# Decode attention over a 65,536-row cache: V's loads issued from ACT's queue, K's from SP's

## The chip, the cores and the metric

The kernel runs on one core of one Trainium2 chip. The metric is the device time of one execution in microseconds (us); lower is better. Engines are named as in the profile: PE (matmul; PEld is its weight load), DVE (vector), ACT (scalar), POOL (GpSimd) and SP (sync). A "q" behind an engine's name is its sequencer, which issues instructions and transfers.

## The reference

One token is decoded by attention over a cache and by a gated feed-forward block; a gate mixes the two. All arrays are bfloat16.

```
x        (1, 1, 512)                 wq (512, 32*128)     wo (32*128, 512)
k_cache, v_cache  (1, 32, 65536, 128)                     gate_w (512)
w_gate, w_up (512, 1792)             w_down (1792, 512)

q = x @ wq, split into 32 heads of 128
for each head: p = softmax(q . K^T / sqrt(128)) over 65536 rows;  o = p @ V
a = concat(o) @ wo
b = (silu(x @ w_gate) * (x @ w_up)) @ w_down
g = sigmoid(sum(x * gate_w))
out = g * a + (1 - g) * b
```

K and V of one head are 16 MB each, and each byte is used once: 32 heads are 1074 MB.

## The kernel before, in words

**Tiles.** Each head's K and V are cut into two parts, u = 0 and u = 1. A part is 256 rows of the cache on each of 128 partitions, 64 KB a partition, 8 MB in all, and is one load (`place`). The text calls the parts of head h K_A(h), K_B(h), V_A(h) and V_B(h).

**Space.** All four lie in one buffer in SBUF, `ring`. K_A takes the bytes 0 to 64 KB of each partition and K_B 32 to 96 KB; V_A takes 96 to 160 KB and V_B 112 to 176 KB. The two parts of K share 32 KB, and those of V share 48 KB, so each load must wait until the part before it has been consumed far enough.

**One head.** DVE transposes a K part in 16 chunks (`turn`, L317) into one of four buffers `kt`, and counts them in the semaphore `ktd`. PE multiplies each chunk with q into `psS` (`scores`, L404) and counts in `qkd`. After both K parts DVE takes the maximum (L341), POOL spreads it over the partitions (L217), ACT forms the exponentials (`softmax`, L252 and L254) and copies the next head's q into `zq` (L259), and DVE transposes the result into `pb` (L343). Then PE multiplies V_A (`flow`, L420), rows 64 to 255 first, after which it raises `va1`. V_B's turn comes in the next head, behind the scores of K_A: PE's block `pe_vb` uses it (L420, then L455 and L411) and raises `vbd`; DVE helps in between (L330, L333) before it turns to K_B. In PE's program the order is thus K_A scores, V_B of the head before, K_B scores, V_A.

**Who issues the loads.** SP issues all of them, on its own queue: wq (L136), then three halves of head 0's K parts at once, then the last half after eight transposes (it carries `s_kb`; the text calls it kb) and V_A(0) (L165), all through the helper at L145. Then `head(r)` runs 31 times, the last time written out. Its waits are these:

- K_A(r+1) after eight transposes of K_B(r)
- V_B(r) after `va1`, which is raised in V_A(r)
- K_B(r+1) after eight transposes of K_A(r+1)
- V_A(r+1) after `vbd`, which is raised in V_B(r)

In the last of them wo is loaded ahead of K_B(31), in two halves, as K_A(31)'s space comes free. After it SP loads w_gate and w_up (once PE is through with wo, `s_wod`), w_down after the last transpose, and V_B(31) in six parts, the last five of them behind `va1`. PE's block `pe_wo`, between V_B(30) and the scores of K_B(31), works on wo; for it ACT copies `om` (L262).

ACT issues three transfers of 1 KB: x, gate_w and the result. `take_q(0)` is its copy of head 0's q (L233), as soon as the projections are through.

Of the kernel before, what the change touches and what calls it, by code (L numbers as in the profile page):

```python
# [9 lines left out]
K_A, K_B = 0, 32 * KB  # L10
V_A, V_B = 96 * KB, 112 * KB
# [15 lines left out]
def bass_gated_mix__mha_block_cached__swiglu_ffn__decode_kernel(  # L27
# [11 lines left out]
    out: bass.AP,  # L39
):  # L40
    _, H, S, Dh = A_k_cache.shape
    D = A_wq.shape[0]
    F = B_w_gate.shape[1]
    Dc = D // P
    FC = F // P
    ROWS = S // (2 * P)
# [8 lines left out]
    with ExitStack() as ctx:  # L55
# [6 lines left out]
        def sem(name):  # L62
            return ctx.enter_context(nc.semaphore(name))
# [47 lines left out]
        sm = {n: sem(n) for n in names.split()}  # L111
# [4 lines left out]
        kv_dram = {"k": A_k_cache[0].rearrange("h (u p r) d -> h u p (r d)", u=2, p=P),  # L116
                   "v": A_v_cache[0].rearrange("h (u p r) d -> h u p (r d)", u=2, p=P)}

        def at(byte, n):
            return ring[:, byte // 2:byte // 2 + n]  # L120
# [15 lines left out]
        nc.sync.dma_start(at(WQ, Dc * H * Dh), A_wq.rearrange("(p c) n -> p (c n)", c=Dc)).then_inc(sm["s_wq"], 16)  # L136
        nc.scalar.dma_start(xrow[0:1, :], xr_dram).then_inc(sm["s_x"], 16)

        body = ExitStack()
        block = body.enter_context(nc.Block())  # L140

        @block.sync
        def _(sp):
            def load(dst, src, s):
                sp.dma_start(dst, src).then_inc(sm[s], 16)  # L145

            def place(kind, h, u, s):
                byte = {"k": (K_A, K_B), "v": (V_A, V_B)}[kind][u]
                src = kv_dram[kind][:, u]
                if isinstance(h, int):  # L150
                    src = src[h]
                else:
                    src = src[bass.ds(h, 1)].rearrange("h p n -> (h p) n")
                load(at(byte, ROWS * Dh), src, s)

            k0 = kv_dram["k"][0, 0]
            k1 = kv_dram["k"][0, 1]
            half = ROWS * Dh // 2
            load(at(K_A + 2 * half, half), k0[:, half:2 * half], "s_ka")
            load(at(K_A, half), k0[:, 0:half], "s_k0a")  # L160
            load(at(K_B + 2 * half, half), k1[:, half:2 * half], "s_k0b")
            sp.wait_ge(sm["ktd"], NCH // 2)
            load(at(K_B, half), k1[:, 0:half], "s_kb")
            sp.wait_ge(sm["s_q"], 1)
            place("v", 0, 0, "s_va")  # L165

            def head(r, late):
                sp.wait_ge(sm["ktd"], r * PER + (PER - NCH // 2))
                place("k", r + 1, 0, "s_ka")
                sp.wait_ge(sm["va1"], r + 1)  # L170
                place("v", r, 1, "s_vb")
                if late:
                    wo_dram = A_wo.rearrange("(p j) n -> p (j n)", j=32)
                    for q in range(2):
                        sp.wait_ge(sm["ktd"], r * PER + (PER + 3 * NCH // 4 + q * NCH // 4))
                        load(at(WO + q * 16 * KB, 16 * D), wo_dram[:, q * 16 * D:(q + 1) * 16 * D], "s_wo")
                sp.wait_ge(sm["ktd"], r * PER + (PER + NCH // 2))
                place("k", r + 1, 1, "s_kb")
                sp.wait_ge(sm["vbd"], r + 2)
                place("v", r + 1, 0, "s_va")  # L180

            with nc.Fori(0, L - 1, engines=[ET.SP]) as i:
                head(i, False)
            head(L - 1, True)
            sp.wait_ge(sm["s_wod"], 1)
            load(at(WG, Dc * F), B_w_gate.rearrange("(p c) f -> p (c f)", c=Dc), "s_wg")
            load(at(WU, Dc * F), B_w_up.rearrange("(p c) f -> p (c f)", c=Dc), "s_wu")
            sp.wait_ge(sm["ktd"], PER * H)
            wd_dram = B_w_down.rearrange("(p c) n -> p (c n)", c=FC)
            load(at(WD, WD_CUT * D), wd_dram[:, 0:WD_CUT * D], "s_wd")  # L190
            last = kv_dram["v"][L, 1]
            for n, ((r0, r1), s) in enumerate(zip(PARTS, MARKS)):
                if n == 1:
                    sp.wait_ge(sm["va1"], H)
                load(at(V_B + r0 * 256, (r1 - r0) * Dh), last[:, r0 * Dh:r1 * Dh], s)
            for j, s in ((FC - 3, "s_wd1"), (FC - 2, "s_wd2"), (FC - 1, "s_wd3")):
                load(at(WD + 2 * j * D, D), wd_dram[:, j * D:(j + 1) * D], s)
# [25 lines left out]
        @block.scalar  # L223
        def _(act):
            chain = [0]

            def link(ins):
                chain[0] += 1
                ins.then_inc(sm["s_ach"], 1)
                act.wait_ge(sm["s_ach"], chain[0])  # L230

            def take_q(h):
                nc.scalar.copy(zq[:, :, 31:128:32], qd[:, h]).then_inc(sm["s_zq"], 1)  # L233

            act.dma_start(gwrow[0:1, :], gw_dram).then_inc(sm["s_x"], 16)
            act.wait_ge(sm["s_zb"], 1)
            nc.scalar.activation(sc[:, 1:2], psQ[:, 1, 0:1], ACT.Exp, scale=-1.0).then_inc(sm["s_e1"], 1)
            for b, bank in enumerate((psY, psZ)):
                act.wait_ge(sm["s_qr"], b + 1)
                nc.scalar.copy(qrow[:, b * D:(b + 1) * D], bank[:]).then_inc(sm["s_qc"], 1)  # L240
            act.wait_ge(sm["s_q"], 1)
            nc.scalar.copy(qTb[:], psM[:, 128:128 + H]).then_inc(sm["s_qTb"], 1)
            act.wait_ge(sm["s_qs"], 1)
            act.wait_ge(sm["s_qd"], 2)
            for g in range(4):
                link(nc.scalar.copy(qd[32 * g:32 * g + 32, :, :, g],
                                    psQ[32 * g:32 * g + 32, :, 0:H].rearrange("p e h -> p h e")))
            take_q(0)

            def softmax(h):  # L250
                act.wait_ge(sm["s_ar"], h + 1)
                nc.scalar.mul(nbias, amx, -SCALE).then_inc(sm["s_nb"], 1)  # L252
                act.wait_ge(sm["s_nb"], h + 1)
                nc.scalar.activation(pa[:], psS[:], ACT.Exp, bias=nbias, scale=SCALE,  # L254
                                     accum_out=rsum).then_inc(sm["s_exp"], 1)

            with nc.Fori(0, L, engines=[ET.Activation]) as i:
                softmax(i)
                nc.scalar.copy(zq[:, :, 31:128:32],  # L259
                               qd[:, bass.ds(i + 1, 1)].rearrange("p a e g -> p (a e) g")).then_inc(sm["s_zq"], 1)  # L260
            act.wait_ge(sm["s_o"], 1)
            nc.scalar.copy(om[:], psQ[:, 0, 0:32]).then_inc(sm["s_om"], 1)  # L262
            act.wait_ge(sm["s_wod"], 1)
            nc.scalar.copy(wo1_ap, psY[:]).then_inc(sm["s_woc"], 1)
            softmax(L)
            act.wait_ge(sm["s_h"], 1)
            nc.scalar.activation(hx[0], psY[:, 0:FW], ACT.Exp, scale=-1.0).then_inc(sm["s_sig"], 1)
            act.wait_ge(sm["s_y"], 1)
            nc.scalar.copy(brow[0:1, :], psF[0:1, :]).then_inc(sm["s_br"], 1)
            act.wait_ge(sm["s_y1"], 1)  # L270
            nc.scalar.copy(fin[0:1, D // 2:D], psZ[64:65, 0:D // 2]).then_inc(sm["s_fin"], 1)
            act.wait_ge(sm["s_fin"], 2)
            act.dma_start(out_dram, fin[0:1, :]).then_inc(sm["s_out"], 16)
# [294 lines left out]
```

## Time and profile before

| | us |
|---|---|
| median of 3 runs | 2513.6 |
| lowest and highest run | 2513.45, 2513.98 |
| the profiled execution's own time | 2514.02 |
| its span, first to last instruction | 2512.5 |
| PE busy | 1481.1 (59%) |
| DVE busy | 1249.7 (50%) |
| ACT busy | 43.0 (2%) |

In rows of the page's groups and of the timeline, L145 is the line of the kernel; `kt<-ring` says which tile is written from which; `x16` is a count. A row of the timeline begins with the start and the duration in us and ends, in brackets, with the idle time of the engine before it and what ended that. A row of the waits gives who waited for whom: the total in us, how often, the longest. A row of the queues gives packets, MB and the share of the 16 engines' time. A row of the DMA issues gives the count, at times the size, and the median time from issue to landing. The granted TensorE clock was 0.781 on the mean.

### The profile page before, as it was taken

What the parts mean: (1) busy time and instruction counts of PE and PEld (TensorE: products, weight loads), DVE (VectorE), ACT (ScalarE), POOL (GpSimd) and SP (SyncE); (2) the same over time, 40 slices, a digit from 0 to 9 for tenths busy, and PEclk for the clock granted to TensorE, in tenths of its full rate; (3) what the DMA queues carried; (4) which work ended last, traced back from release to release, by engine and by line L of the source; (5) the groups of instructions that cost most, each with busy time, mean ns of one, the idle gap of its engine ahead of it and who ended that gap; (6) DMA issues with size and microseconds to landing.
All of it is one profiled execution on the core that took longest, in us unless ns stands there. A gap on an engine that the chain in (4) does not pass through costs nothing.

```text
span 2512.5 us, 25156 instructions
## 1 busy us (share of the span) xinstructions
PE 1481.1 (59%) x10029; PEld 575.0 (23%) x10158; DVE 1249.7 (50%) x1213; ACT 43.0 (2%) x142; POOL 25.8 (1%) x81
## 2 busy tenths in 40 slices
PE   4664655645646546556465574564655655656568
PEld 1222222212212222222222221222222222222222
DVE  5463553644545536446455364464553644645534
ACT  0000000000000000000000000000000000000000
POOL 0000000000000000000000000000000000000000
PEclk8787877878778777777787787877877778778788
DMA  9999999999999999999999999999999999999999
GB/s 418 434 434 434 434 434 434 434 434 434 434 434 434 434 434 434 434 434 434 434 434 434 434 434 435 436 435 434 435 437 435 435 435 434 434 436 434 434 434 392
DMA packets 20746, 1087.71 MB, mean 433 GB/s; under 512 B 2307, under 2 KB 2694, under 8 KB 2950
## 3 DMA queue, kind: packets, MB, share of 16 engines
q1 hardware_dynamic: 20736, 1087.64, 100.0%
q8 instruction: 4, 0.07, 0.0%
q10 hardware_dynamic: 6, 0.00, 0.0%
HBM read 1087.64 MB, written 0.00 MB: 433 GB/s over the span
## 4 chain that ended last, share of the span: by engine, by line
DMA 75%; DVE 16%; issue 7%; PE 1%; DVEq 1%; SPq 0%; ACT 0%; POOL 0%
DMA ring<-in_A_k_cache_dram 74%; DVE kt L317 15%; PE psS L404 1%; DMA ring<-in_A_v_cache_dram 1%; DVEq L314 0%; SPq L145 0%; PE psW L420 0%; DVE st L328 0%; PE psY L426 0%; PE psO L411 0%; ACT pa L254 0%; DVE pb L343 0%; DVE st L341 0%; DVEq L327 0%; DVE fin L362 0%
## 5 line engine op out<-in xcount | busy, mean ns | idle before, releaser
L317 DVE STREAM_TRANSPOSE kt<-ring 128x1024 uint32<-128x1024 uint32 x1024 | 1163.2, 1206 | 932.4 <-DMA ring<-in_A_k_cache_dram 932.4
L404 PE MATMUL psS<-kt,zq 128*128 128x512 bf16 x3968 | 1103.3, 423 | 881.1 <-DVE kt L317 858.5
L404 PEld LDWEIGHTS psS<-kt,zq 128*128 128x128 bf16 x4096 | 387.1, 105 | 1583.7 <-DVE kt L317 1120.8
L420 PE MATMUL psW<-ring,pb 128*4 128x512 bf16 x3584 | 253.8, 445 | 102.8 <-DVE pb L343 102.4
L420 PEld LDWEIGHTS psW<-ring,pb 128*4 128x4 bf16 x3584 | 94.0, 98 | 260.8 <-issue 184.7
L330 DVE COPY brow<-psW 128x512 f32<-128x512 f32 x32 | 22.1, 690 | 120.3 <-PE psW L420 120.3
L411 PEld LDWEIGHTS psO<-pb,ring 128*128 128x128 bf16 x2048 | 57.0, 98 | 0.5 <-DMA ring<-in_A_v_cache_dram 0.3
L411 PE MATMUL psO<-pb,ring 128*128 128x1 bf16 x2048 | 56.6, 163 | 0.3 <-DMA ring<-in_A_v_cache_dram 0.2
L333 DVE TENSOR_SCALAR lt<-psO,st,sc 128x4 f32 x32 | 9.4, 293 | 92.6 <-PE psO L411 92.6
L455 PE MATMUL psO<-id,brow 128*128 128x1 f32 x256 | 33.7, 253 | 25.5 <-DVE brow L330 24.7
L343 DVE STREAM_TRANSPOSE pb<-pa 128x512 bf16<-128x512 bf16 x32 | 22.8, 712 | 48.7 <-ACT pa L254 48.7
L252 ACT ACTIVATE st<-st 128x1 f32<-128x1 f32 x32 | 6.5, 203 | 2354.5 <-POOL st L217 2354.5
L341 DVE TENSOR_REDUCE st<-psS 128x1 f32<-128x512 f32 x32 | 22.1, 692 | 37.5 <-PE psS L404 37.5
L455 PEld LDWEIGHTS psO<-id,brow 128*128 128x128 f32 x256 | 31.0, 191 | 41.7 <-DVE brow L330 40.4
L217 POOL PARTITION_ALL_REDUCE st<-st x32 | 11.2, 350 | 2416.5 <-DVE st L341 2416.5
L254 ACT ACTIVATE pa<-psS,st 128x512 bf16<-128x512 f32 x32 | 22.0, 687 | 1.0
L431 PE MATMUL psF<-ring,om 128*1 (+1 forms) x32 | 12.9, 403 | 3.1 <-DMA ring<-in_A_wo_dram 2.6
L516 PE MATMUL psY<-ring,hot 128*128 (+1 forms) x31 | 12.7, 409 | 0.0
L219 POOL PARTITION_ALL_REDUCE st<-st x32 | 12.3, 383 | 36.4 <-ACT pa L254 36.4
L259 ACT COPY zq<-qd 128x16 bf16 x31 | 7.7, 248 | 0.0
L431 PE MATMUL psF<-ring,kt 128*1 128x512 bf16 x11 | 4.9, 630 | 3.0 <-DVE kt L356 3.0
L254 ACT ACTIVATION_READ_ACCUMULATOR pa<-psS,st 128x1 f32 x32 | 6.2, 193 | 0.0
(87 smaller groups left out, 53.1 us busy)
## 6 DMA issues: line engine op xcount, KB each, us to landing
ring<-in_A_k_cache_dram SPq DMA_DIRECT2D x4, 4096.0 KB, 27.5
ring<-in_A_v_cache_dram SPq DMA_DIRECT2D x3, 2048.0 KB, 17.4
ring<-in_A_wq_dram SPq DMA_DIRECT2D x1, 4096.0 KB, 12.1
ring<-in_A_wo_dram SPq DMA_DIRECT2D x2, 2048.0 KB, 10.4
ring<-in_B_w_gate_dram SPq DMA_DIRECT2D x1, 1792.0 KB, 20.9
ring<-in_B_w_up_dram SPq DMA_DIRECT2D x1, 1792.0 KB, 24.8
ring<-in_B_w_down_dram SPq DMA_DIRECT2D x1, 1408.0 KB, 12.9
ring<-in_A_v_cache_dram SPq DMA_DIRECT2D x1, 1280.0 KB, 21.1
```

The source lines that it names most:

```text
L219: nc.gpsimd.partition_all_reduce(Lt, rsum, P, RADD).then_inc(sm["s_L"], 1)
L254: nc.scalar.activation(pa[:], psS[:], ACT.Exp, bias=nbias, scale=SCALE, accum_out=rsum).then_inc(sm["s_exp"], 1)
L317: nc.vector.transpose(o, src).then_inc(sm["ktd"], 1)
L330: nc.vector.tensor_copy(brow[:], psW[:]).then_inc(sm["s_flc"], 1)
L341: nc.vector.reduce_max(mxs, psS[:], AX_X).then_inc(sm["s_mx"], 1)
L343: nc.vector.transpose(pb[:], pa[:]).then_inc(sm["s_pb"], 1)
L404: last = nc.tensor.matmul(psS[:], zw[je][c], ktb[n % NB][:, je // 2, :, je % 2], start=first and je == 0, stop=stop and je == 3)
L411: last = nc.tensor.matmul(psO[:, 0:1], at(base + r * 256, Dh), pb[:, col:col + 1], start=first and n == 0, stop=stop and n == len(rows) - 1)
L420: last = nc.tensor.matmul(psW[g:g + 4, :], pb[:, col:col + 97:32], at(base + r * 256, 4 * Dh), start=first and n < 4, stop=stop and n >= l ...
L431: return nc.tensor.matmul(psF[0:1, :], lhs, rhs, start=first, stop=stop)
L455: nc.tensor.matmul(psO[:, 0:1], brow[:, e * Dh:(e + 1) * Dh], id4[:, e:e + 1], start=e == 0, stop=False)
L516: return nc.tensor.matmul(psY[:], hot[:, bass.ds(31 - j, P)], w, start=first, stop=stop)
```

## The change

V's 8 MB loads leave SP's program for ACT's. `place` becomes a helper of both and takes the issuing engine. ACT issues V_A(0) behind `take_q(0)`, without the wait for the last K half, and in each of its 31 rounds, behind the softmax and the copy of `zq`, waits for `va1`, issues V_B(i), waits for `vbd` and issues V_A(i+1). SP keeps K, the weights and the six parts of V_B(31), with their waits, and loses the four lines with V's waits and loads. Sizes, places in `ring`, semaphores and the other engines' programs stay as they are.

```diff
+        def place(eng, kind, h, u, s):
+            byte = {"k": (K_A, K_B), "v": (V_A, V_B)}[kind][u]
+            src = kv_dram[kind][:, u]
+            if isinstance(h, int):
+                src = src[h]
+            else:
+                src = src[bass.ds(h, 1)].rearrange("h p n -> (h p) n")
+            eng.dma_start(at(byte, ROWS * Dh), src).then_inc(sm[s], 16)
...
         def _(sp):
...
             sp.wait_ge(sm["ktd"], NCH // 2)
             load(at(K_B, half), k1[:, 0:half], "s_kb")
-            sp.wait_ge(sm["s_q"], 1)
-            place("v", 0, 0, "s_va")
 
             def head(r, late):
                 sp.wait_ge(sm["ktd"], r * PER + (PER - NCH // 2))
-                place("k", r + 1, 0, "s_ka")
-                sp.wait_ge(sm["va1"], r + 1)
-                place("v", r, 1, "s_vb")
+                place(sp, "k", r + 1, 0, "s_ka")
                 if late:
...
                 sp.wait_ge(sm["ktd"], r * PER + (PER + NCH // 2))
-                place("k", r + 1, 1, "s_kb")
-                sp.wait_ge(sm["vbd"], r + 2)
-                place("v", r + 1, 0, "s_va")
+                place(sp, "k", r + 1, 1, "s_kb")
...
             take_q(0)
+            place(act, "v", 0, 0, "s_va")
...
                 softmax(i)
                 nc.scalar.copy(zq[:, :, 31:128:32],
                                qd[:, bass.ds(i + 1, 1)].rearrange("p a e g -> p (a e) g")).then_inc(sm["s_zq"], 1)
+                act.wait_ge(sm["va1"], i + 1)
+                place(act, "v", i, 1, "s_vb")
+                act.wait_ge(sm["vbd"], i + 2)
+                place(act, "v", i + 1, 0, "s_va")
             act.wait_ge(sm["s_o"], 1)
```

More of the change, by code (lines that the diff above doesn't have):

```diff
@@ L145, in load @@
                 sp.dma_start(dst, src).then_inc(sm[s], 16)
[L147 to L154, printed above, removed]
             k0 = kv_dram["k"][0, 0]
```

## The prediction

> **What bounds the kernel now.** I read the page first: the span, the rate by slices, the queues and the chain that ended last.
>
> ```profile
> span 2512.5 us, 25156 instructions
> GB/s 418 434 434 434 434 434 434 434 434 434 434 434 434 434 434 434 434 434 434 434 434 434 434 434 435 436 435 434 435 437 435 435 435 434 434 436 434 434 434 392
> q1 hardware_dynamic: 20736, 1087.64, 100.0%
> q10 hardware_dynamic: 6, 0.00, 0.0%
> DMA 75%; DVE 16%; issue 7%; PE 1%; DVEq 1%; SPq 0%; ACT 0%; POOL 0%
> ```
>
> 38 of 40 slices run at 434 to 437 GB/s, and SP's queue (q1) carries all of 1087.64 MB. At 434.4 GB/s that is 2503.8 us of the span of 2512.5. So the transfers are the bound, and they hardly ever stop. The chain's 16% DVE is no cost of its own: the engines go on moving V there. A microsecond in which no load is in flight is a microsecond of the result, and hardly more can be gained than the 8.7 us between these two numbers. ACT's queue (q10) carried three loads or stores of 1 KB.
>
> Then the waits, all engines and SP's queue:
>
> ```profile
> ACT st L252 <- POOL st L217: 2354.5, 32, 76.5
> DVE kt L317 <- DMA ring<-in_A_k_cache_dram: 932.4, 65, 22.3
> PEld psW L420 <- DMA ring<-in_A_v_cache_dram: 14.6, 32, 0.9
> SPq L145 <- DVE kt L317: 1367.2, 65, 30.9
> SPq L145 <- PE psW L420: 537.1, 32, 18.2
> SPq L145 <- PE psO L411: 476.9, 31, 15.8
> ```
>
> DVE waits for K; V arrives just in time (14.6 us over 32 waits). SP waits for consumers to free space, always with loads already queued. ACT is idle some 76 us per head.
>
> Last the timeline of one head. It has four loads of 8 MB, two of K and two of V.
>
> ```profile
> 621.50 0.33 SPq L145 DMA_DIRECT2D ring<-in_A_v_cache_dram  x1
> 633.12 1.25 DVE L317 STREAM_TRANSPOSE kt<-ring 128x1024 uint32<-128x1024 uint32 x1 [16.49 <-DMA ring<-in_A_k_cache_dram]
> 642.48 0.33 SPq L145 DMA_DIRECT2D ring<-in_A_k_cache_dram  x1
> 652.38 2.26 PEld L420 LDWEIGHTS psW<-ring,pb 128*4 128x4 bf16 x48 [0.44 <-DMA ring<-in_A_v_cache_dram]
> 658.65 0.33 SPq L145 DMA_DIRECT2D ring<-in_A_v_cache_dram  x1
> 671.68 18.14 DVE L317 STREAM_TRANSPOSE kt<-ring 128x1024 uint32<-128x1024 uint32 x16 [12.50 <-DMA ring<-in_A_k_cache_dram]
> 680.99 0.33 SPq L145 DMA_DIRECT2D ring<-in_A_k_cache_dram  x1
> 694.18 3.13 PEld L420 LDWEIGHTS psW<-ring,pb 128*4 128x4 bf16 x64 [3.75 <-issue]
> 697.15 0.33 SPq L145 DMA_DIRECT2D ring<-in_A_v_cache_dram  x1
> ```
>
> K lands at 633.12 and again at 671.68, a half-head of 38.6 us, so one load takes 19.3 us of all engines. Counted from K's landing, three things happen in each half: at 9.3 us eight transposes are done and the next K is issued (642.48 and 680.99); PE takes up V at 19.3 (652.38) or 22.5 (694.18); at 25.5 us V's space is free and the next V is issued (658.65 and 697.15). In one queue these loads land strictly in turn: K, V, K, V.
>
> **The change, part by part.** *The issues.* 63 loads of V leave SP for ACT, at 0.33 us each on SP. ACT's 76 us of idle time a head hide two of them, whichever engine's price holds. The two new waits (va1, vbd) stand behind the softmax and the copy of zq. Behind them on ACT is only the next softmax, which begins after all of K_B's scores, long after vbd in the rows above (V's issue at 658.65, K_B's landing at 671.68). Price: 0. After the last head's vbd ACT also owes PE the copy of om; one issue of 0.33 us stands ahead of it, hidden by the wait for wo. *SP* no longer passes the V waits, but they ended before K's (621.50 ahead of 642.48, 658.65 ahead of 680.99), so K leaves at the same events: 0. The issue gains nothing, then; what changes is the order of service.
>
> *Two queues instead of one.* Does a load on ACT's queue wait behind what SP has queued?
>
> ```profile
> 0.73 0.39 SPq L136 DMA_DIRECT2D ring<-in_A_wq_dram  x1
> 1.17 32.69 SPq L145 DMA_DIRECT2D ring<-in_A_k_cache_dram  x4
> 1.28 0.21 ACTq L235 DMA_DIRECT2D gwrow<-in_gate_w_dram  x1
> 8.05 0.68 DVE L302 CUSTOM_DVE_ANT_0 xg<-xrow,gwrow 1x512 f32<-1x512 bf16 x1 [4.63 <-DMA gwrow<-in_gate_w_dram]
> 12.99 1.90 PE L384 MATMUL psY<-ring,xTz 128*32 128x512 bf16 x16 [3.62 <-DMA ring<-in_A_wq_dram]
> 19.98 0.26 ACT L233 COPY zq<-qd 128x16 bf16<-128x16 bf16 x1
> 33.53 19.48 DMA ring<-in_A_k_cache_dram
> 33.91 0.44 SPq L145 DMA_DIRECT2D ring<-in_A_v_cache_dram  x1
> 62.44 29.18 DMA ring<-in_A_k_cache_dram
> ring<-in_A_wq_dram SPq DMA_DIRECT2D x1, 4096.0 KB, 12.1
> ring<-in_A_v_cache_dram SPq DMA_DIRECT2D x63, 32.2
> ```
>
> gate_w, issued at 1.28 on ACT, was there at 8.05, while wq, issued before it on SP, came at 12.99 with three K halves behind it. So the engines interleave the queues. K and V loads have the same shape, so I take equal shares while both are in flight. No row shows two bulk queues: the share could be anything between 0 and 1, and these ends stay in the rivals. Equal is my estimate, from the equal shapes alone. The Trainium skill, "DMA: Bandwidth & Descriptors", section "Queues, rings and completion order", says that each engine goes round robin between queues, a packet at a time; by that too the shares are equal, and gate_w's row agrees as far as it goes.
>
> The joint rate I leave at 434. The bounds are the 418 and the 437 of single slices; the 418 is the start-up, the 437 one slice in forty, so 434 is the nearest row.
>
> *Steady state.* In a half-head V is alone from 0 to 9.3, then both run until V lands at x, then K alone until 25.5, then both until 38.6. V's 19.3 us of engine time: 13.1/2 + 9.3 + (x - 9.3)/2, so x = 16.2. K's: 6.9/2 + 9.3 + 13.1/2 = 19.3, so K still lands after 38.6. V lands 3.1 us before PE wants it (19.3), and something is always in flight. Price: 0 per head, with a cover of 3.1 us; if it goes, see the second rival.
>
> *Start.* V_A(0) now goes out as the zq copy ends, at 20.24, not at 33.91 behind the last K half (kb). Before, kb landed at 33.53 + 19.48 = 53.0. The first load of head 1's K landed at 62.44 + 29.18 = 91.6, so everything ahead of it was through at 91.6 - 19.3 = 72.3. V_A(0) at half rate needs 38.6 us and ends near 60; K's halves, slowed by it, end last: kb lands at 72.3, when nothing else is queued. K_A(1) is issued after eight transposes, at 81.6, and V_B(0) only after the softmax. A load alone also has a lead: wq took 12.1 us where 4096 KB at 434 GB/s are 9.7, so 2.4 us. The engines stand still 9.3 + 2.4 = 11.7 us. Before, V_A(0) covered this gap. Bounds: 0, if kb still lands by 60.6, and 11.7.
>
> *Tail.* Rows of the timeline around the last head:
>
> ```profile
> 2410.44 1.25 DVE L317 STREAM_TRANSPOSE kt<-ring 128x1024 uint32<-128x1024 uint32 x1 [16.47 <-DMA ring<-in_A_k_cache_dram]
> 2424.16 4.83 SPq L145 DMA_DIRECT2D ring<-in_A_wo_dram  x2
> 2429.04 0.43 SPq L145 DMA_DIRECT2D ring<-in_A_k_cache_dram  x1
> 2435.95 0.33 SPq L145 DMA_DIRECT2D ring<-in_A_v_cache_dram  x1
> 2458.79 18.14 DVE L317 STREAM_TRANSPOSE kt<-ring 128x1024 uint32<-128x1024 uint32 x16 [22.31 <-DMA ring<-in_A_k_cache_dram]
> 2461.30 0.33 SPq L145 DMA_DIRECT2D ring<-in_B_w_gate_dram  x1
> 2476.96 0.33 SPq L145 DMA_DIRECT2D ring<-in_B_w_down_dram  x1
> 2477.33 10.50 SPq L145 DMA_DIRECT2D ring<-in_A_v_cache_dram  x6
> ```
>
> I count from the landing of K_A(31), 2410.44. Before, V_B(30) had its 19.3 us still to go there. Now it has moved half of 13.1 already and is through at 12.7. wo is issued at 13.7 (2424.16): a gap of 1.0 + 2.4 = 3.4 us. wo's two halves (4.83 us each) end at 25.8; K_B, issued at 18.6, follows alone until V_A, issued at 25.5, joins at 27.9. K_B has 17.2 of its 19.3 left, at half rate 34.4: it lands at 62.3, against 48.3 before (2458.79). V_A ends 2.1 later, at 64.4, and w_gate with w_up (3584 KB, 8.4 us, issued near 50 as in 2461.30) at 72.8; then nothing is queued. w_down and the last V wait for the end of K_B's transposes, 2476.96 - 2458.79 = 18.2 after its landing, at 80.5: a gap of 7.7 + 2.4 = 10.1. w_down and the first V part cover 8.1 us, to 91.0. The other five parts wait for va1, which the block of six issues (10.50 us) puts some 8.6 after w_down's, at 89.1, plus the lead 91.5: 0.5. Together 14.0 us. Bounds: 0, if K_B gets at least 0.7 of the engines, to 26.7, if V_B(30) has nothing left at 0 and the first gap becomes 13.7 + 2.4.
>
> *Sum.* 0 (issues) + 0 (31 heads) + 11.7 + 14.0 = 25.7. On the profiled execution's own time, 2514.0 (span 2512.5 and 1.5 around it), that is 2539.7. The median of the runs is 0.4 lower, so I say 2539.
>
> **The rivals.** *Turns by whole loads.* If an engine finishes one queue's load before it takes the other's, the steady state stays K, V, K, V, and the tail as it was. V_A(0) still goes ahead of kb, so the 11.7 remain: 2525. For it speaks that gate_w took 6.8 us for 1 KB, a good part of a load; against it, that it came before wq's end.
>
> *V is late.* If K gets more than half, V's landing x moves: with share s for K, 9.3 + 10/(1 - s) - 13.1. At s = 0.57 it is 19.4, PE's time; beyond, PE waits for V, in program order ahead of K_B's scores, DVE stops with it, K_B lies there landed and the next K is not issued. Then nothing is in flight while PE works on V: 6.3 us (652.38 to 658.65) and 3.0 us (694.18 to 697.15), with 2.4 lead each 14.1 us a head, 437 us over 31 heads: 2976, with all values between for a loss in some heads only. For it speaks the small cover of 3.1 us; against it, the equal loads.
>
> *Not slower: the longer queue gets more turns.* If the share of K rises with what SP has queued, the covers remain: it would need 0.81 at the start (K's queue, through at 53.0 before, has 31.4 us left when V's bytes begin near 21.6, and kb would have to land by 60.6) and 0.7 in the tail, where K_B, w_gate and w_up queue together (17.2 us of K_B between 27.9 and 52.2), but at most 0.57 in the heads, where one load stands against one. Then the time is 2514 and no difference. The Trainium skill, "DMA: Bandwidth & Descriptors", section "Issuing engines are not separate DMA queues", says that issuing from several engines only saves issue time; taken as the whole story it gives the same 2514. Against it speaks that one queue served its loads in order (wq alone, in 12.1 us, with three more loads queued), so queued loads don't ask for turns.
>
> **How the numbers follow.** Equal shares with the cover holding 0.68, own range 2528 to 2556 (the bounds of start and tail); whole loads 0.10; V late 0.17, most of it above 2590; not slower 0.05. The range of 2522 to 2590 leaves out the last case and most of V late. A measurement of this kernel can tell about 0.2% (5 us) from no change. Faster needs a rate above any slice here: 0.02; same 0.04; slower 0.94.
>
> **What would show it.** Right: q10 carries 63 loads (about 528 MB) and the mean rate of the middle slices stays at 434; the first and last slices drop (11.7 us without transfers between 72 and 85, about 10 before w_down); kb lands at 72 and K_B(31) 14 us later after K_A(31) than before; ACT's waits cost nobody. The steady state is wrong if the middle slices fall or PE's wait for V at L420 grows from 14.6 us into hundreds. The share is wrong if V's median landing, 32.2 us before, isn't near 29 (13.1 + 16.2); the whole account is wrong if the time rises with all slices at 434, or if the joint rate differs from it.

## The result and the profile after

The median rose from 2513.7 us to 2544.1 us (2540.8 to 2546.7): a ratio of 1.012, interval 1.0103 to 1.0138. The profiled execution took 2540.8 us, the least of them. It is set against the profiled 2514.0 of before; its span is 26.9 us longer. Lines of the kernel have moved a little: the transposes are L316, the flow matmuls L419, both queues' 8 MB loads L146.

The page after, and of its DMA issues the row of V on ACT's queue (count, median us from issue to landing):

```profile
span 2539.4 us, 25193 instructions
GB/s 421 344 441 429 430 441 434 430 429 444 430 430 436 439 430 429 444 430 430 438 437 430 429 445 430 429 444 430 430 430 444 430 429 444 430 430 432 443 427 305
q1 hardware_dynamic: 11664, 559.16, 51.0%
q10 hardware_dynamic: 9078, 528.49, 48.0%
...
ring<-in_A_v_cache_dram ACTq DMA_DIRECT2D x63, 29.7
```

The same bytes move, V's on q10. Two slices have sunk, the second (434 to 344 GB/s) and the last (392 to 305); those between lie at 427 to 445, around the same 434. Windows show where the transfers stop; the last number of a row is GB/s, the one before it the share of the engines. First the kernel before from 72 to 84 us, then the kernel after:

```profile
72.00:84.00 12.00, 6.88 (x66) 2.04 (x64) 1.40 (x2) 1.13 (x4) 0.73 (x2) 0.72 1.00 433
```

```profile
60.00:72.00 12.00, 3.66 (x16) 1.40 (x15) 2.88 (x4) 0.00 (x0) 0.00 (x0) 0.87 0.82 354
72.00:84.00 12.00, 9.91 (x34) 3.97 (x36) 11.62 (x11) 0.00 (x0) 0.00 (x0) 0.70 0.26 87
400.00:1000.00 600.00, 346.95 (x2402) 134.97 (x2434) 292.74 (x282) 9.03 (x32) 5.87 (x16) 0.77 1.00 435
1000.00:2300.00 1300.00, 769.87 (x5236) 299.85 (x5302) 656.78 (x628) 19.20 (x68) 12.47 (x34) 0.78 1.00 434
2480.00:2505.00 25.00, 14.17 (x51) 5.53 (x54) 15.99 (x15) 0.00 (x0) 0.00 (x0) 0.68 0.73 315
2505.00:2517.00 12.00, 8.71 (x88) 2.90 (x92) 3.82 (x6) 0.98 (x3) 0.73 (x2) 1.00 0.73 289
```

Measured against 434 GB/s, the two windows at the start lose 2.2 + 9.6 = 11.8 us. From 400 to 2300 us nothing is lost. A window counts each row of a load (one partition's share of it, one packet in the trace's records) whole at the row's start. Spread over the time that each row took, 2.42 us for 64 KB, the records give 13.0 us lost between 60 and 100 us, nothing between 100 and 2380 us that the kernel before doesn't lose too, and 13.9 us more than before from there to the end: together the 26.9. The waits after:

```profile
ACT st L247 <- POOL st L211: 2388.2, 32, 76.2
DVE kt L316 <- DMA ring<-in_A_k_cache_dram: 940.9, 65, 37.5
PEld psW L419 <- DMA ring<-in_A_v_cache_dram: 17.0, 6, 2.9
```

ACT is as idle as before, so the issues and waits it took over cost nobody. PE's wait for V is 17.0 us instead of 14.6. DVE's longest wait for K went from 22.3 us to 37.5: that is K_B(31). Now the timeline at the start:

```profile
20.11 0.36 ACTq L146 DMA_DIRECT2D ring<-in_A_v_cache_dram  x1
24.18 1.25 DVE L316 STREAM_TRANSPOSE kt<-ring 128x1024 uint32<-128x1024 uint32 x1 [14.37 <-DMA ring<-in_A_k_cache_dram]
52.98 9.13 DVE L316 STREAM_TRANSPOSE kt<-ring 128x1024 uint32<-128x1024 uint32 x8 [19.60 <-DMA ring<-in_A_k_cache_dram]
72.38 18.14 DVE L316 STREAM_TRANSPOSE kt<-ring 128x1024 uint32<-128x1024 uint32 x16 [9.50 <-DMA ring<-in_A_k_cache_dram]
81.69 153.51 SPq L146 DMA_DIRECT2D ring<-in_A_k_cache_dram  x5
97.80 37.97 ACTq L146 DMA_DIRECT2D ring<-in_A_v_cache_dram  x2
```

kb lands at 72.4 and K_A(1) is issued at 81.69, with V_B(0) not yet due: the last row ends at 71.9, the next begins at 82.7, and nothing moves for some 11 us. The second K half, due 9.7 us after the first alone, came 28.8 us after it (24.18 to 52.98): three times as long, beside V_A(0). K's halves have rows of 32 KB and V of 64 KB, so one row of each in turn gives K a third. The rows of the queues from 28 to 48 us, V's queue (q10) and K's (q1), come close to that:

```profile
q10 hardware_dynamic: 91, 5.96, 68.8%
q1 hardware_dynamic: 80, 2.62, 30.3%
```

And the end:

```profile
2425.49 1.25 DVE L316 STREAM_TRANSPOSE kt<-ring 128x1024 uint32<-128x1024 uint32 x1 [14.00 <-DMA ring<-in_A_k_cache_dram]
2439.21 4.83 SPq L154 DMA_DIRECT2D ring<-in_A_wo_dram  x2
2451.14 0.34 ACTq L146 DMA_DIRECT2D ring<-in_A_v_cache_dram  x1
2489.01 18.14 DVE L316 STREAM_TRANSPOSE kt<-ring 128x1024 uint32<-128x1024 uint32 x16 [37.48 <-DMA ring<-in_A_k_cache_dram]
2507.18 0.33 SPq L154 DMA_DIRECT2D ring<-in_B_w_down_dram  x1
```

K_B(31) lands 63.5 us after K_A(31) (48.3 before), and w_down leaves at 81.7 after it (66.5 before), when nothing else is in flight. Here K_B(31) and V_A(31) stand side by side, both with rows of 64 KB, and from 2456 to 2484 us they share evenly:

```profile
q1 hardware_dynamic: 96, 6.29, 51.8%
q10 hardware_dynamic: 93, 6.09, 50.2%
```

(These rows too count whole at the start, so a sum can pass 100%.)

### The profile page after: what moved, and what is told of

Read it like the earlier page. It is cut to its first block, busy times and chain, and to the rows that moved or that the text cites. A ratio compares the mean times of both kernels' runs of the same rounds, so it can differ in the third digit from the quotient of the medians.

```text
span 2539.4 us, 25193 instructions
## 1 busy us (share of the span) xinstructions
PE 1488.6 (59%) x10029; PEld 576.3 (23%) x10158; DVE 1249.7 (49%) x1213; ACT 43.0 (2%) x142; POOL 25.8 (1%) x81
## 4 chain that ended last, share of the span: by engine, by line
DMA 74%; DVE 16%; issue 7%; PE 2%; DVEq 1%; SPq 0%; ACT 0%; POOL 0%
DMA ring<-in_A_k_cache_dram 74%; DVE kt L316 15%; PE psS L403 1%; DVEq L313 1%; PE psW L419 0%; PE psF L430 0%; SPq L146 0%; DVE st L327 0%; PE psY L490 0%; DVE kt L350 0%; PE psO L410 0%; PE psY L425 0%; PE psO L454 0%; ACT pa L249 0%; DVE pb L342 0%
## 5 line engine op out<-in xcount | busy, mean ns | idle before, releaser
L316 DVE STREAM_TRANSPOSE kt<-ring 128x1024 uint32<-128x1024 uint32 x1024 | 1163.1, 1205 | 940.9 <-DMA ring<-in_A_k_cache_dram 940.9
L419 PE MATMUL psW<-ring,pb 128*4 128x512 bf16 x3584 | 259.6, 453 | 116.3 <-DVE pb L342 102.3
L419 PEld LDWEIGHTS psW<-ring,pb 128*4 128x4 bf16 x3584 | 95.5, 99 | 277.3 <-issue 201.0
## 6 DMA issues: line engine op xcount, KB each, us to landing
ring<-in_B_w_gate_dram SPq DMA_DIRECT2D x1, 1792.0 KB, 20.3
```

Source lines behind the costliest of these rows:

```text
L316: nc.vector.transpose(o, src).then_inc(sm["ktd"], 1)
L419: last = nc.tensor.matmul(psW[g:g + 4, :], pb[:, col:col + 97:32], at(base + r * 256, 4 * Dh), start=first and n < 4, stop=stop and n >= l ...
```

## The experiments

**V_A(0) back on SP.** The other 62 V loads stay on ACT.

```diff
             load(at(K_B, half), k1[:, 0:half], "s_kb")
+            sp.wait_ge(sm["s_q"], 1)
+            place(sp, "v", 0, 0, "s_va")
...
             take_q(0)
-            place(act, "v", 0, 0, "s_va")
```

> Only V_A(0) goes back to SP's queue, behind the last K half (kb), as in the kernel before; every other V load stays on ACT. Theory (the loss is two stretches without transfers, one at each end, because V shares the engines with a K load that somebody waits for): kb lands near 53 again instead of 72, K_A(1) is issued near 62.4, the empty stretch at 72 to 82 is gone, and the time falls by 10.8 to 11.7 us from the changed kernel's 2544, to about 2533. Rival (two queues cost a little in every head, and the stretch at the start is made up for later): the time falls by less than 4 us and the later heads lose what the start gains.

Measured: 2535.0 us, 9.1 less. Its timeline:

```profile
53.33 18.14 DVE L317 STREAM_TRANSPOSE kt<-ring 128x1024 uint32<-128x1024 uint32 x16 [9.42 <-DMA ring<-in_A_k_cache_dram]
62.63 48.69 SPq L146 DMA_DIRECT2D ring<-in_A_k_cache_dram  x2
101.62 1.25 DVE L317 STREAM_TRANSPOSE kt<-ring 128x1024 uint32<-128x1024 uint32 x1 [26.06 <-DMA ring<-in_A_k_cache_dram]
```

kb is back at 53 and the gap at 72 is gone. The gain is some 2 us short of the expected, and the third row shows why: K_A(1), 91.6 in the kernel before, now lands at 101.6, because V_B(0), the first load on ACT, takes its share from it. More on this below.

**V_A(0) on ACT, but issued late.**

```diff
             take_q(0)
+            act.wait_ge(sm["ktd"], NCH // 2)
             place(act, "v", 0, 0, "s_va")
```

> V_A(0) stays on ACT's queue but is issued at the time the kernel before issued it, after eight transposes (near 34 us instead of 20). Theory (sharing between queues, by rows of unequal size, so V's 64 KB rows get the greater part beside K's 32 KB rows): V still passes k0b and kb, kb still lands near 72, nothing gained, 2540 to 2546. Rival (the engines serve loads by the time of their issue, and the harm is that V_A(0) is issued 14 us early): kb is ahead of V, lands near 53, and about 11 us are gained, near 2533.

Measured: 2545.6 us, nothing gained.

```profile
33.56 0.37 ACTq L146 DMA_DIRECT2D ring<-in_A_v_cache_dram  x1
72.44 18.14 DVE L317 STREAM_TRANSPOSE kt<-ring 128x1024 uint32<-128x1024 uint32 x16 [28.71 <-DMA ring<-in_A_k_cache_dram]
```

Issued with kb, V still passes it, and kb lands at 72.4 as if V had left at 20. The rival falls: the harm at the start comes from the second queue, not from the earlier issue.

**V_A(31) back on SP.**

```diff
             head(L - 1, True)
+            sp.wait_ge(sm["vbd"], L + 1)
+            place(sp, "v", L, 0, "s_va")
...
-            with nc.Fori(0, L, engines=[ET.Activation]) as i:
+            with nc.Fori(0, L - 1, engines=[ET.Activation]) as i:
...
+            softmax(L - 1)
+            take_q(L)
+            act.wait_ge(sm["va1"], L)
+            place(act, "v", L - 1, 1, "s_vb")
```

> Only V_A(31) goes back to SP's queue, behind K_B(31), as in the kernel before; V_A(0) and all other V loads stay on ACT. Theory: K_B(31) doesn't share any more, lands 33 to 36 us after K_A(31)'s transposes allow its issue at most (48 us after K_A(31) landed instead of 62), the empty stretch of 8.6 us ahead of w_down goes, and from the landing of K_A(31) to the end it takes 102 us as before instead of 114: about 12 us less, near 2532. Rival (w_gate, w_up and the six V parts are what is late, whatever V_A(31) does): less than 4 us gained.

Measured: 2530.6 us, 13.5 less than with all V on ACT.

```profile
2432.72 1.25 DVE L322 STREAM_TRANSPOSE kt<-ring 128x1024 uint32<-128x1024 uint32 x1 [16.39 <-DMA ring<-in_A_k_cache_dram]
2478.37 18.14 DVE L322 STREAM_TRANSPOSE kt<-ring 128x1024 uint32<-128x1024 uint32 x16 [19.62 <-DMA ring<-in_A_k_cache_dram]
2496.54 0.33 SPq L154 DMA_DIRECT2D ring<-in_B_w_down_dram  x1
```

K_B(31) lands 45.7 us after K_A(31) and w_down leaves at 63.8. One load moved from one queue to the other takes away the tail's loss; the rival falls.

**Both back on SP,** the two edits together.

> Both edits: V_A(0) and V_A(31) on SP, the 61 other V loads on ACT. Theory (no loss in the 31 heads between): both empty stretches go, 2513 to 2521, and the runs lie as close together as those of the kernel before (0.5 us) if the spread of 6 us of the changed kernel comes from its two ends. Rival (the heads themselves lose by two queues, V late in some of them): 2525 or more, with PE's wait for V above the 15 us of before.

Measured: 2522.1 us (2520.3 to 2523.7, ratio 1.0033, interval 1.0021 to 1.0046). The two gains add up (9.1 + 13.5 against 22.0), but 8.4 us remain, between the two expectations, and the runs still spread by 3.4 us, so the spread doesn't come from the two ends alone. The heads between don't have the 8.4 us (the rate is that of before, and PE's wait for V is 18.1 us in all):

```profile
100.00:130.00 30.00, 23.03 (x184) 9.60 (x184) 19.19 (x19) 0.00 (x0) 0.00 (x0) 0.84 0.92 391
400.00:1000.00 600.00, 355.06 (x2404) 137.08 (x2404) 301.81 (x289) 7.90 (x28) 5.13 (x14) 0.77 1.00 435
1000.00:2300.00 1300.00, 775.83 (x5269) 296.94 (x5268) 647.11 (x619) 19.18 (x68) 12.46 (x34) 0.77 1.00 434
```

From 100 to 130 us the rate is 391. K_A(1) and V_B(0) share, so K_A(1) lands at 101.4 instead of 91.6 and K_B(1) is issued only at 110.75; V_B(0)'s last row ends at 110.6, and for a moment nothing moves.

**Four V loads on SP,** V_A(0), V_B(0), V_B(30) and V_A(31): as the last, with these lines more.

```diff
-            def head(r, late):
+            def head(r, late, vb=False):
...
                 place(sp, "k", r + 1, 0, "s_ka")
+                if vb:
+                    sp.wait_ge(sm["va1"], r + 1)
+                    place(sp, "v", r, 1, "s_vb")
...
+            head(0, False, True)
...
-            head(L - 1, True)
+            head(L - 1, True, True)
```

ACT's rounds 0 and 30 are written out without these two loads.

> V_A(0), V_B(0), V_B(30) and V_A(31) on SP, the 59 other V loads on ACT: one more load at each end than in the run that gave 2522 with V_A(0) and V_A(31). Theory (the 8 us that were left there are the price of going over from one queue to two and back: the first V load on ACT takes half the engines from a K load that DVE waits for, wherever that is): the cost moves one load later and stays, 2519 to 2524. Rival (it is V_B(0) beside K_A(1) and V_B(30) ahead of wo in particular): 2514 to 2516.

Measured: 2517.1 us (ratio 1.0015, interval 1.0006 to 1.0025): between the two, so each held for one end. Going over to two queues had its price here too; the timeline shows that it moved on to K_B(1):

```profile
91.89 1.25 DVE L329 STREAM_TRANSPOSE kt<-ring 128x1024 uint32<-128x1024 uint32 x1 [16.39 <-DMA ring<-in_A_k_cache_dram]
140.12 18.14 DVE L329 STREAM_TRANSPOSE kt<-ring 128x1024 uint32<-128x1024 uint32 x16 [22.14 <-DMA ring<-in_A_k_cache_dram]
```

K_A(1) is in time again and K_B(1) comes 48.2 us after it instead of 38.6. At the other end there was no price of going back: with V_B(30) on SP ahead of wo that loss is gone (433 GB/s from 2400 to 2510 us, 420 in the run before it). What remains, 3.3 us, is the entry.

**V's loads cut in four.** This tests the shares, and the second rival's price. The waits on V's semaphores count four landings in place of one.

```diff
-            eng.dma_start(at(byte, ROWS * Dh), src).then_inc(sm[s], 16)
+            cut = 4 if kind in "v" else 1
+            w = ROWS * Dh // cut
+            for c in range(cut):
+                eng.dma_start(at(byte + 2 * c * w, w), src[:, c * w:(c + 1) * w]).then_inc(sm[s], 16)
```

> The changed kernel with each of ACT's V loads cut into four loads of 16 KB rows instead of one of 64 KB rows (K keeps 64 KB rows; the first part of V_B(31) is cut in four as well, for the count of its semaphore). Theory (the engines take the queues in turn, a row at a time, so the share goes by the size of the rows): V gets 16 of 80 parts, 0.2, while K is in flight. V starts near 29 us after K's landing, moves 0.2 x 7 = 1.4 us of its 19.3 beside K, 15 alone, and needs 13 us more for the rest: it lands at 28 instead of the 19.3 at which PE wants it, PE waits for V in each head, and the cover is gone: 2700 to 2980, with PE's wait for V in the hundreds. Rival (equal shares in time whatever the rows, or loads in turn): 2541 to 2548 as with whole loads.

Measured: 3075.3 us. Its waits, its windows, its timeline around 1000 us, and the queues from 1020 to 1044 us, while K and V are both in flight:

```profile
PEld psW L424 <- DMA ring<-in_A_v_cache_dram: 1421.6, 61, 25.2
```

```profile
1000.00:2300.00 1300.00, 634.68 (x4312) 239.56 (x4305) 531.25 (x509) 15.80 (x56) 10.28 (x28) 0.71 0.82 349
```

```profile
911.50 18.13 DVE L321 STREAM_TRANSPOSE kt<-ring 128x1024 uint32<-128x1024 uint32 x16
1007.05 18.13 DVE L321 STREAM_TRANSPOSE kt<-ring 128x1024 uint32<-128x1024 uint32 x16
```

```profile
q1 hardware_dynamic: 132, 8.26, 79.4%
q10 hardware_dynamic: 143, 2.08, 20.3%
```

V gets a fifth, as expected from 16 KB against 64. A head takes 95.6 us instead of 77.3. PE waits for V 61 times, and behind each wait K's turn stops too, so that the rate falls to 349. The sign and the mechanism are those expected; the size is not, for 3075 lies above the range of 2700 to 2980. The prediction had put the price at 14.1 us a head, and it is 18.3.

**Both kinds cut in four** (`"kv"` in place of `"v"`).

> As the run before it, but K's 62 loads on SP are cut into four loads of 16 KB rows too, so both queues have rows of one size again. Theory (the share goes by the ratio of the rows, and the cut itself costs nothing): equal shares, the cover of the heads is back, 2541 to 2550. Rival (smaller rows, or four times as many loads and issues, are what costs): as slow as the run with V alone cut, 2700 or more.

Measured: 2554.7 us. Its waits and windows:

```profile
PEld psW L424 <- DMA ring<-in_A_v_cache_dram: 52.3, 18, 5.9
```

```profile
1000.00:2300.00 1300.00, 782.09 (x5177) 297.38 (x5178) 656.45 (x627) 19.19 (x68) 12.49 (x34) 0.78 1.01 431
```

With rows of one size the loss of 531 us is gone, but for 10.6: so it was the ratio of the rows, not their size. It lies 5 us above the expected range, because the cut does cost something: the heads run at 431 GB/s with rows of 16 KB, which is 0.7% of some 2240 us, or about 15 us. The start gives some 4 of them back: beside K's halves with their 32 KB rows, V's 16 KB rows get 33.6% from 28 to 48 us, and kb lands at 68.0 instead of 72.4.

**K alone cut in four** (`"k"`).

> The changed kernel with only K's 62 loads on SP cut into four loads of 16 KB rows; V keeps 64 KB rows on ACT. Theory (shares by the size of the rows, and either queue can starve the other): K gets 0.2 while V is in flight, V's 19.3 us take 24, K's last 7 us are stretched to 26, so K lands near 57 after the K before it instead of 38.6, together with V, and nothing is in flight until eight transposes are done, some 10 us in each half-head: 2900 to 3200, with DVE's wait for K well above 940 and PE's wait for V near nothing. Rival (only V's cover of 3 us counts, and K's share is V's gain): 2541 to 2556, no slower than with both cut.

Measured: 2839.5 us, less than expected and far above the rival. Its waits and timeline:

```profile
DVE kt L319 <- DMA ring<-in_A_k_cache_dram: 1263.6, 65, 40.6
PEld psW L422 <- DMA ring<-in_A_v_cache_dram: 16.4, 7, 2.6
```

```profile
1047.73 18.14 DVE L319 STREAM_TRANSPOSE kt<-ring 128x1024 uint32<-128x1024 uint32 x16 [29.63 <-DMA ring<-in_A_k_cache_dram]
1078.87 1.25 DVE L319 STREAM_TRANSPOSE kt<-ring 128x1024 uint32<-128x1024 uint32 x1 [8.90 <-DMA ring<-in_A_k_cache_dram]
1136.89 18.14 DVE L319 STREAM_TRANSPOSE kt<-ring 128x1024 uint32<-128x1024 uint32 x16 [30.13 <-DMA ring<-in_A_k_cache_dram]
```

DVE waits for K and PE hardly for V, as the theory has it. K's share, from 1110 to 1134 us, is 20.1%. But only every second K is late: the distances are 31.1 and 58.0 us here, so this head takes 89.2. The expectation had all of them at 57.

No version here beats the kernel before, in whose span 2503.8 of 2512.5 us are bytes at 434.4 GB/s.

## Why the prediction was right

The forecast was 2539 and the median is 2544.1; for the profiled execution it was 2539.7, and that took 2540.8.

*Issues and waits: 0.* They held; ACT's and PE's waits above.

*Start: 11.7 us.* The windows give 11.8, the rows with their durations 13.0. kb at 72.3 (72.4 measured) and the issue at 81.6 (81.69) came out to a tenth, although the share was wrong there: V_A(0) took two thirds, not half. It didn't matter, because kb ends with the last of a fixed amount of bytes as long as V isn't slower than K (with V's rows cut to 16 KB it is, and kb lands at 68.0). The run with V_A(0) on SP shows that this loss hangs on that load, and the late issue that it is the queue.

*Heads: 0.* The price held: 434 GB/s from 400 to 2300 us, and V lands ahead of PE's turn (at 1053.7 us, 16.8 after K, 16.2 by the working; PE takes it up at 19.3). The way there was another. The working had both queues at work for 20 of the 38.6 us of a half-head. In the records, rows of K and of V stand side by side for 6.9 us of it on the mean; the rest of the time one queue has all engines. The queues from 1012 to 1029 us, then from 1035 to 1049:

```profile
q1 hardware_dynamic: 112, 7.34, 99.6%
```

```profile
q10 hardware_dynamic: 96, 6.29, 103.6%
```

A load's rows begin 3.4 to 3.9 us after its issue, and its landing is signalled 2.8 us after its last row (last section). Counted for K and for V, these delays are 12.9 us a half-head, which is what the overlap lacks (20 less 6.9), so that in the heads the loads nearly take turns, K, V, K, V, as in one queue. The working had neither delay. V's median landing, 29.7 us after its issue against 29.3, is therefore in part luck. The condition, equal shares for equal rows, was an estimate from shapes. The tail shows it directly, and the cut loads from both sides: with a fifth for V or a fifth for K the heads break, and with equal rows, whole or cut, they don't.

*Tail: 14.0 us.* The end lost 13.9 us, K_B(31) at 62.3 (63.5 measured) and w_down at 80.5 (81.7) held, and moving V_A(31) gave 13.5. That the sum came out so closely is luck, for two errors cancel. By the rows with their durations, the gap ahead of w_down cost 10.4 us (10.1 forecast) and the one ahead of the last five parts 0.6 (0.5). But the first gap, ahead of wo, was put at 3.4 us and cost 1.0. The overlap of V_B(30) with K_A(31) was reckoned from V's issue, at 2417.20; its first row moved at 2421.26, so V had more left to move, and it covered most of the gap. On the other side, the stretch behind the last loads, for which the working had no term, grew by 1.9 us; the cause stays open.

*What the sum lacked.* It had no term for the way from the start into the steady state, and none for spread. The entry costs some 3 us in the run with four loads on SP; the profiled execution of the changed kernel paid nothing for it. This differs from run to run: between 100 and 400 us, in one profile each, the rate is 434 GB/s in the profiled execution of the changed kernel (2540.8), 431 in that of the late issue (2545.2) and 429 in that with V_A(31) on SP (2535.4, whose other runs lie at 2530 to 2531); 429 instead of 434 are 3.5 us. Why one run settles sooner than another stays open. The own range of 2528 to 2556 doesn't follow from the bounds of start and tail that it names: they span 0 to 38.4 us, so 2514 to 2552.

*The rivals.* Turns by whole loads: fallen as a rule of the engines, for a K half beside V took three times its time, K_B(31) and V_A(31) shared evenly, and cutting V would not have mattered; that the heads come near to turns has the other reason given above. V is late: its mechanism is real, and it begins where rows differ; its size was 18.3 us a head, not 14.1. The longer queue gets more turns: fallen, K's queued halves got less than V's single load, not more. The Trainium skill, "DMA: Bandwidth & Descriptors", has two sentences here that point apart. "Issuing engines are not separate DMA queues" says that a second issuing engine saves only issue time; for bandwidth the runs agree (434 GB/s), for time they don't (+30 us). "Queues, rings and completion order" has the engines go round robin by packets; the runs agree, if a packet is a row of the load (32 KB against 64: 30.3%; 16 against 64: 20.3%; 64 against 64: half).

## What to carry to other kernels

Where transfers bound a kernel, a second queue adds no bandwidth but changes who lands when: of two loads that share, the first lands later than it would have in one queue, and its successor is issued later. Look at the places where the next issue hangs on a landing, above all first and last loads, and keep there in one queue, in the order of need, what in the middle may stand in two. The share goes by the size of the rows of the loads, so cutting one stream finer hands the engines to the other.

## What was not expected of the hardware

A load starts later while the other queue is at work, and its landing is signalled later too. In the trace's records of single rows, the first row of K_A(1), issued at 81.69 with nothing in flight, moves 1.0 us after its issue; that of V_B(30), issued at 2417.20 beside K, after 4.1 us, and that of a K load issued at 1007.61 beside V after 3.4. The medians are 3.4 us for K and 3.9 for V. The landing follows the last row by 2.8 us in the heads, where in the kernel before it was 0.3.

The run with both kinds cut, whose rows of 16 KB took 0.61 us instead of 2.42, tells the two delays apart. There the landing follows the last row by 0.96 us. In both runs that is about one row more than with one queue, as if the signal waited for a row of the other queue. The start doesn't fit this: with the short rows it is still 3.4 us. What it waits for isn't shown.

Rows of 16 KB ran at 431 GB/s where rows of 64 KB ran at 434.
